# Attention on one core: per-rotation semaphores and group order for the first two heads, other shares of VectorE and GpSimd per head

## The chip, the cores and the metric

The kernel runs on one core of a Trainium2 chip. The metric is the device time of one execution in microseconds (us); the kernel before takes 672.16 us, the median of three runs (672.07 to 673.51). Times inside the kernel come from the profile of one execution, whose span is 670.2 us.

## The reference

Attention with normalised queries and keys: 32 heads, 2048 rows, 20 elements in each row, in bfloat16.

```python
qn = q / (sqrt((q*q).sum(-1)) + eps)
kn = k / (sqrt((k*k).sum(-1)) + eps)
logits = einsum('bhqd,bhkd->bhqk', qn, kn) * t[None, :, None, None]
attn = softmax(logits)
out  = einsum('bhqk,bhkd->bhqd', attn, v)
```

There are 32 x 2048 x 2048 exponentials to take, and a row has only 20 elements, so the exponentials and not the products are the bulk of the work.

## The kernel before, in words

**Units.** Scores are made transposed: keys on the 128 partitions, queries along the free axis. One unit is 128 keys by 512 queries; a head has 16 key blocks r and 4 query groups g, so 64 units. A row has 20 elements, padded to 32, so four of them fit on the 128 partitions: the query tile `qz` is block-diagonal, group g on partitions 32g to 32g+31. A key block r sits on the partitions of group r mod 4. When r mod 4 is not g, the keys must be on other partitions, so three rotated copies of the keys exist (`kR`, rotation dl = (r - g) mod 4 = 1, 2, 3; rotation 0 is `qkT` itself).

**Two engines take exponentials.** Of the 16 key blocks of a head, ScalarE takes 11 or 12 (`A_units`), VectorE 4 or 5 (`D_tiles`, of four units each). The list `DVE_TILES` says how many, by head. ScalarE works in waves of 2 and 3 units in turn: TensorE writes the scores of a wave into one of two slots of `psA`, ScalarE writes the exponentials into the ring `p_ring` (line 757). For VectorE, TensorE writes half a tile, 1024 scores on each of the 128 partitions, into `psD`; VectorE converts it to int16 so that the bits read as float16 are a rough exponential (`xt`, line 803); then three shifts of these integers (`ss`, line 815 on VectorE, line 821 on GpSimd) are combined by TensorE with values `vph` scaled for each shift. There is one `psD` buffer, four `xt` buffers and three of each `ss`. The first two shifts of a tile run on VectorE. The third runs on GpSimd for the first tiles of a head, as many as `KDN` says, and on VectorE for the rest.

**Output.** TensorE accumulates value products of all kinds in `psO` (line 686); when a head is finished, VectorE transposes (line 699), takes the reciprocal of the sum (702), GpSimd or VectorE multiplies (710), and a DMA stores it.

**Preparation of a head.** Loads of q, k and v; squares (527), sums (529), an inverse square root in five or six small steps (532 to 550) on VectorE; the multiplication on GpSimd (562), or on VectorE for heads 1 and 2 (569). Then the SP queue issues a DMA transpose into `qkT` (580), four copies that make `qz`, and six copies that make the three rotations in `kR`, two for each. Head 0 is prepared in its own way, with transposes on TensorE. Heads 1 and 2 are prepared alone, later ones in pairs.

**What sets the order.** All operations are tasks with an engine, an assumed duration, dependences and a due time. When the program is built, `list_schedule` places them with an assumed clock, and each engine then runs its list in that order, in order, with the semaphore waits of `plan_waits`. So a constant of the planner, or a due time, can move instructions anywhere in the kernel. The constants named in the diff: `SWITCH` is a penalty for changing the kind of matmul, `SPARE` the slack that a score matmul must have before it is turned into a slower, fuller form, `DSL` an allowance added to VectorE's backlog when TensorE chooses between scores for ScalarE and for VectorE, `LEAD` how many heads ahead the preparation is due, `DLEAD` how much of a head ahead VectorE's tiles are due.

**Head 0 and the others.** Head 0 visits its units diagonal by diagonal: all units of rotation 0 first, then rotation 1 and so on. The other heads go by key blocks, so their first four units already need all rotations. The semaphore of a copy into `kR` is one for all six (line 590), and the wait of a score matmul is

```python
if h:
    return [trn[h]] + rot[h]      # rot[h]: four qz copies, then six kR copies
```

Of the kernel before, what the change touches and what calls it, by code (L numbers as in the profile page):

```python
# [43 lines left out]
class Program:  # L44
# [2 lines left out]

    SEM_LAT = {"PE": 0.20, "ACT": 0.17, "DVE": 0.14, "POOL": 0.15, "SP": 0.0}

    SWITCH = 0.3  # L50
    LIGHT = 9.0
    TICK = 3.41
    LOAD = 3500.0
# [1 line left out]
    PE_REST = 4.2  # L55
    PV_SLACK = 0.6
    OVER = 0.03
    SPARE = 0.05
    DSL = 0.4
    HOLDA = 9.0  # L60
    HPE = 0.1
    HOLD = {"DVE": 0.0, "PE": HPE}
# [5 lines left out]
    def add(self, eng, name, fn, dur, deps=(), pri=0.0, lat=0.0, dma=None):  # L68
        t = Task(eng, name, fn, dur, deps, pri, lat, dma)
        self.tasks.append(t)  # L70
        return t

    def schedule(self):
# [4 lines left out]
        for _ in range(self.PASSES):  # L78
# [7 lines left out]
            for j, t in enumerate(pe):  # L86
# [3 lines left out]
                for tier in range(3):  # L90
                    m = j - 1
                    while i and load < self.LOAD and m >= i:
                        u = pe[m]
                        if u.modes and u not in heavy and u not in more and (
                                tier == 2 or u.modes[1][2] == u.dur or tier == 1 and
                                u.modes[1][2] - u.dur <= min(v.start for v in u.users) - u.end - 0.2 - self.SPARE):
                            more.add(u)
# [13 lines left out]
    def list_schedule(self):  # L111
# [80 lines left out]
        while events or ready["POOL"]:  # L192
# [13 lines left out]
            for e in touched:  # L206
# [14 lines left out]
                if e == "PE":  # L221
                    if self.DSL is not None and any(r[2].name[0] == "q" for r in ready[e]):
                        more = sum(r[2].dur for r in ready["DVE"]) + self.DSL
                        x = min((r for r in ready[e] if r[2].name[0] == "q"), key=lambda r: (
                            (free["ACT"] if r[2].name[2] == "A" else free["DVE"] + more) - r[2].dur, r[0], r[1]))
                    else:
                        x = min(ready[e], key=lambda r: (r[0] + (0.0 if r[2].name[:2] == last_pe[0] else self.SWITCH), r[1]))
                    ready[e].remove(x)
# [93 lines left out]
def bass_standalone__qk_norm__prompt_kernel(  # L322
# [7 lines left out]
    B, H, S, D = q.shape  # L330
    assert B == 1 and D == 20 and S == 2048, (B, H, S, D)
    R = S // 128
    NG = 4
    WAVES = (2, 3)
    GORD = (0, 2, 1, 3)
# [4 lines left out]
    NV = 6  # L340
# [6 lines left out]
    NWARM = 14  # L347
    EARLY = 3
    NSOLO = 3
    LEAD = 2.9  # L350
    SPREAD = 1.0
    FIRST = -7.0
    DLEAD = 0.9
    PE_MM = 0.23
    MORE = 25
    DVE_TILES = [4 + (h * MORE // 31 > (h - 1) * MORE // 31 if h else 0) for h in range(H)]
    NDMAX = 6
    NPOOL, FPOOL = True, True
    SQPOOL = False
# [1 line left out]
    TTRATE = 0.00168  # L361
    TTDUR, TTWIN = 0.8, 0.55
    NCH = 1
    KDN = (3,)
    PCH, PRATE = 512, 0.00164
    SHP = 0.0

    with ExitStack() as es:
# [11 lines left out]
        vph = [sbuf(f"vph{i}", [128, len(PHASES), NDMAX, 32], FP16) for i in range(NV)]  # L380
# [21 lines left out]
        def dma(eng, name, dst, src, deps, pri, key, lat=2.2, dur=0.65):  # L402
            return add(eng, name, lambda e, tk: e.dma_start(dst, src), dur, deps, pri, lat=lat, dma=key)  # L403
# [5 lines left out]
        A_units, D_tiles = [], []  # L409
        for h in range(H):  # L410
            nd = DVE_TILES[h]
            na = R - nd
            if h == 0:

                A_units += [(0, 4 * c + (g + dl) % 4, g) for dl in range(4) for c in range(3) for g in GORD]
                A_units += [(0, 12 + (g + dl) % 4, g) for dl in range(nd, 4) for g in GORD]
            else:
                A_units += [(h, r, g) for r in range(na) for g in GORD]

            if h == 0:  # L420
                D_tiles += [(0, [12 + (g + dl) % 4 for g in range(NG)]) for dl in range(R - na)]
            else:
                D_tiles += [(h, [r] * NG) for r in range(na, R)]
        NA = len(A_units)
        nA_head = [(R - DVE_TILES[h]) * NG for h in range(H)]
        a0 = [sum(nA_head[:h]) for h in range(H + 1)]
        d0 = [sum(DVE_TILES[:h]) for h in range(H + 1)]
        waves = []
# [32 lines left out]
        lds, ld_v, norm, trn, rot = {}, {}, {}, {}, {}  # L461
# [10 lines left out]
        def add_loads(h):  # L472
            b, bv = h % NB, h % NV
            pri = h - LEAD - 0.5
            war = (norm[h - NB] if h >= NB else []) + ([lambda: [trn[max(0, h - 4)]]] if h >= EARLY else [])
            x = qk_sb[b]
            lds[h] = [dma("SP", f"ldk{h}", x[:, R:2 * R, :], k[0, h].rearrange("(p r) d -> p r d", p=128),
                          war, pri - 0.01 if h else -50, f"k{b}", lat=4.5 if h else 2.2)]
            if h == 0:
                lds[h].append(dma("ACT", "ldq0", x[:, 0:R, :], q[0, 0].rearrange("(p r) d -> p r d", p=128),  # L480
                                  [], -99, "q0a"))
            else:

                for nh in range(4):
                    src = bass.AP(q.tensor, q[0, h].offset + nh * D,
                                  [[16 * D, 32], [4 * D, 4], [512 * D, 4], [1, D]])
                    dst = x[32 * nh:32 * nh + 32, 0:R, :].rearrange("p (c g) d -> p c g d", g=4)
                    lds[h].append(dma("SP", f"ldq{h}", dst, src, war, pri, f"q{b}", lat=4.5))
            war = (pv_users[h - NV] if h >= NV else z_v[bv]) + ([lambda: [trn[h - 2]]] if h >= 2 else [])
            if h == 1:  # L490
                war = war + [lambda: [trn[0]]]
            ld_v[h] = dma("SP", f"ldv{h}", vaug[bv][:, :, 0:D], v[0, h].rearrange("(p r) d -> p r d", p=128),
                          war, pri + 0.1, f"v{bv}", lat=3.0)
            nd = NDMAX if h == 0 else DVE_TILES[h]
            vsc[h] = [add("POOL", f"vs{h}", lambda e, tk, i=i: e.tensor_scalar(  # L495
                vph[bv][:, i, 0:nd, :], vaug[bv][:, R - nd:R, :], 2.0 ** (-PHASES[i] / 1024.0), 1.0, ALU.mult, ALU.mult),
                0.4, [ld_v[h]] + (pv_users[h - NV] if h >= NV else z_v[bv]), pri + 0.2) for i in range(len(PHASES))]
            for u in vsc[h] if h else []:
                u.win = 0.14

        def add_prep(hs):
            due = hs[0] - LEAD if hs[0] != 1 else FIRST
            n = len(hs)
# [72 lines left out]
        def add_trn(h):  # L576
            b, bt = h % NN, h % NT
            due = h - LEAD
            war = [lambda: qk_users[h - NT] + rot[h - NT]] if h >= NT else []
            trn[h] = add("SP", f"trn{h}", lambda e, tk: e.dma_start_transpose(  # L580
                qkT[bt][:, :].rearrange("p (c n) -> p c n", n=128),
                qkn[b][:, :, :].rearrange("p r d -> p (r d)")), 1.3, norm[h] + war, due + 0.1, lat=3.0, dma=f"T{bt}")
            rot[h] = [dma("SP", f"qz{h}", qz[bt][32 * g:32 * g + 32, g, :], qkT[bt][32 * g:32 * g + 32, 0:512],
                          [trn[h], z_qz[bt]] + ([lambda: qk_users[0]] if h == NT else []), due + 0.15, f"Z{bt}") for g in range(NG)]

            for dl in range(1, 4):
                m = 128 - 32 * dl
                for (d, s, n) in ((0, 32 * dl, m), (m, 0, 32 * dl)):
                    rot[h].append(dma("SP", f"rot{h}", kR[bt][d:d + n, dl - 1, :], qkT[bt][s:s + n, 512:1024],
                                      [trn[h]], due + 0.2, f"R{bt}"))  # L590

        warm = []
        for i in range(NWARM):
# [75 lines left out]
        def qk_deps(units):  # L669
            h = units[0][0]  # L670
            if h:
                return [trn[h]] + rot[h]
            return ([head0[0]] if all(r < 8 and r % 4 == g for _, r, g in units) else [trn[0]]) + [q0[g] for _, _, g in units] + [rot[0][dl - 1] for dl in sorted({(r - g) % 4 for _, r, g in units}) if dl]

        first_pv = {}
# [1 line left out]
        def pv_mm(eng, h, r_of, rhs_of, phase=None):  # L677
            start = h not in first_pv
            first_pv[h] = True
            last = None  # L680
            for g in range(NG):
                if phase is None:
                    w = vaug[h % NV][:, r_of(g), :]
                else:
                    w = vph[h % NV][:, phase, r_of(g) - (R - (NDMAX if h == 0 else DVE_TILES[h])), :]
                last = eng.matmul(psO[32 * g:32 * g + 32, :], w, rhs_of(g), start=start,  # L686
                                  stop=False, skip_group_check=True, tile_position=(0, 32 * g))
            return last
# [38 lines left out]
        def add_wave(w):  # L727
# [14 lines left out]
            for h in hs:  # L742
                deps += qk_deps([A_units[u] for u in us if A_units[u][0] == h])
# [31 lines left out]
        def add_dgroup(jg):  # L775
# [5 lines left out]
            for i, j in enumerate(js):  # L781
                h, rg = D_tiles[j]
                due = h + (j - d0[h] + 0.3) / DVE_TILES[h] - DLEAD
                n1 = W1 // 512
# [24 lines left out]
            def dv(name, fn, dur, deps):  # L809
                return add("DVE", f"{name}{js[0]}", fn, 0.068 + dur * len(js), deps, due)  # L810
            sh = []
            for i in range(len(PHASES)):
                dst, war = ss[i][se], t1s + old(f"s{i}", NE)
                if i < 2 or jg < 2 or js[0] - d0[D_tiles[js[0]][0]] >= KDN[D_tiles[js[0]][0] % len(KDN)]:
                    sh.append([dv(f"s{i}.", lambda e, tk, i=i, dst=dst: e.tensor_scalar(  # L815
# [97 lines left out]
```

## Time and profile before

| engine | busy us | share of the span |
|---|---|---|
| TensorE matmul (PE) | 614.8 | 92% |
| VectorE (DVE) | 655.9 | 98% |
| ScalarE (ACT) | 657.3 | 98% |
| GpSimd (POOL) | 350.0 | 52% |

The largest groups of the page: the exponentials on ScalarE (line 757) 650.1 us in 575 instructions; the conversions on VectorE (803) 371.5 us in 306; the shifts on VectorE (815) 242.1 us in 365; the half shifts on GpSimd (821) 234.6 us in 188. In a row of the timeline the columns are start, duration, engine, line, operation, output and input, and in brackets the idle time of the engine before it with what ended that. In a row of the waits they are the engine and line that waited, what it waited for, the total in us, how often, and the longest. In a row by stretches of time they are the busy time of TensorE, its weight loads, VectorE, ScalarE and GpSimd, then the granted TensorE clock as a share of full speed, and the DMA engines' share and rate. The DMA issues of the page give 1.9 us from issue to landing for a `qz` copy and 1.9 to 2.2 us for a `kR` copy.

### The profile page before, as it was taken

To read this page: it belongs to the slowest core of one execution; us is meant where nothing else is said; L and a number is where in the kernel's file an instruction comes from. 1 tells how busy PE (TensorE), PEld (TensorE's weight loads), DVE (VectorE), ACT (ScalarE), POOL (GpSimd) and SP (SyncE) were. 2 spreads that over 40 slices of the span, in tenths; PEclk is the share of its full clock that TensorE was granted. 3 is DMA by queue.
4 is the path that set the end of the run, shared out by engine and by line. 5 is a ranking of instruction groups with operands and counts; after the bars stand their busy time and mean duration, and the time that the engine had idled before them with its cause. 6 is when DMAs were issued, how large, how long until landed. Compare 5 with 4: busy or idle time off the path is not lost.

```text
span 670.2 us, 14522 instructions
## 1 busy us (share of the span) xinstructions
PE 614.8 (92%) x5959; PEld 167.2 (25%) x5959; DVE 655.9 (98%) x927; ACT 657.3 (98%) x584; POOL 350.0 (52%) x364
## 2 busy tenths in 40 slices
PE   8799989999999899899989999999999999999997
PEld 2222222222222222222222222222222222222221
DVE  8979999999999999999999999999999999999997
ACT  9789999999999999999999999999999999999997
POOL 2335555565545546566465645646456456554522
PEclk9979999999999999999999999999999999999999
DMA  5552614425342351333424243352413424130200
GB/s 63 69 76 43 88 18 90 41 57 75 43 80 23 67 64 30 77 36 86 46 48 76 34 85 30 67 65 44 81 17 84 51 41 80 21 86 10 52 8 11
DMA packets 196722, 36.22 MB, mean 54 GB/s; under 512 B 172592, under 2 KB 196656, under 8 KB 196656
## 3 DMA queue, kind: packets, MB, share of 16 engines
q1 hardware_dynamic: 196512, 35.22, 33.7%
q8 instruction: 46, 0.75, 0.5%
q14 instruction: 20, 0.16, 0.1%
q10 hardware_dynamic: 144, 0.08, 0.0%
HBM read 7.87 MB, written 2.62 MB: 16 GB/s over the span
## 4 chain that ended last, share of the span: by engine, by line
ACT 88%; DVE 7%; PE 3%; SPq 1%; DMA 1%; issue 1%
ACT p_ring L757 88%; DVE xt L803 3%; DVE ss L815 2%; PE psA L667 1%; PE psO L594 1%; SPq L403 1%; PE psO L686 1%; DMA qkT<-qkn 0%; PE psD L667 0%; DMA kR<-qkT 0%; DVE rs_sum L529 0%; DVE sq L527 0%; DVE qz L638 0%; DVE oT L699 0%; DVE kx L646 0%
## 5 line engine op out<-in xcount | busy, mean ns | idle before, releaser
L757 ACT ACTIVATE p_ring<-psA 128x1024 bf16<-128x1024 f32 (+1 forms) x575 | 650.1, 1373 | 7.0 <-PE psA L667 7.0
L803 DVE TENSOR_SCALAR xt<-psD 128x1024 int16<-128x1024 f32 x306 | 371.5, 1214 | 7.4 <-PE psD L667 6.5
L821 POOL TENSOR_TENSOR ss<-xt,two 128x512 int32<-128x512 int32 x188 | 234.6, 1248 | 161.4 <-DVE ss L815 80.9
L667 PE MATMUL psA<-qz,kR 32*128 32x512 bf16 (+2 forms) x1077 | 236.8, 386 | 33.6 <-ACT p_ring L757 25.8
L815 DVE TENSOR_SCALAR ss<-xt 128x2048 int16<-128x2048 int16 x365 | 242.1, 683 | 1.2
L686 PE MATMUL psO<-ss,vph 128*32 128x512 f16 x1836 | 171.6, 385 | 0.9 <-DVE ss L815 0.9
L686 PE MATMUL psO<-p_ring,vaug 128*32 128x512 bf16 x1436 | 134.1, 384 | 0.0
L667 PE MATMUL psA<-qz,qkT 64*128 64x512 bf16 (+2 forms) x359 | 121.9, 386 | 10.9 <-ACT p_ring L757 9.4
L667 PE MATMUL psD<-qz,kR 64*128 64x512 bf16 (+1 forms) x459 | 126.1, 386 | 3.9 <-DVE xt L803 2.2
L667 PEld LDWEIGHTS psA<-qz,kR 32*128 32x128 bf16 (+2 forms) x1077 | 55.1, 92 | 184.0 <-ACT p_ring L757 176.4
L495 POOL TENSOR_SCALAR vph<-vaug 128x160 f16<-128x160 bf16 (+2 forms) x96 | 40.2, 419 | 99.7 <-DMA vaug<-in_v_dram 39.0
L686 PEld LDWEIGHTS psO<-ss,vph 128*32 128x32 f16 x1836 | 44.8, 94 | 80.2 <-issue 60.6
L562 POOL TENSOR_TENSOR qkn<-qk_sb,rs_r 128x640 bf16<-128x640 bf16 x29 | 46.8, 1615 | 34.2 <-DVE ss L815 24.2
L686 PE MATMUL psO<-xt,vaug 128*32 128x512 f16 x612 | 60.7, 387 | 0.0
L667 PE MATMUL psD<-qz,qkT 64*128 64x512 bf16 (+1 forms) x153 | 58.6, 387 | 0.8 <-DVE xt L803 0.6
L686 PEld LDWEIGHTS psO<-p_ring,vaug 128*32 128x32 bf16 x1436 | 35.5, 94 | 51.9 <-issue 45.5
L667 PEld LDWEIGHTS psD<-qz,kR 64*128 64x128 bf16 (+1 forms) x459 | 30.4, 93 | 66.8 <-DVE xt L803 50.6
L667 PEld LDWEIGHTS psA<-qz,qkT 64*128 64x128 bf16 (+2 forms) x359 | 29.2, 92 | 58.2 <-ACT p_ring L757 56.7
L710 POOL TENSOR_TENSOR o_stage<-oT,rec 128x320 bf16<-128x320 f32 x30 | 26.0, 866 | 15.3 <-DVE ss L815 12.9
L529 DVE TENSOR_REDUCE rs_sum<-sq 128x32 f32<-128x640 bf16 x32 | 25.5, 802 | 0.1
L686 PEld LDWEIGHTS psO<-xt,vaug 128*32 128x32 bf16 x612 | 15.8, 93 | 34.1 <-issue 26.8
L699 DVE STREAM_TRANSPOSE oT<-psO 128x512 f32<-128x512 f32 x32 | 22.6, 707 | 0.8 <-PE psO L686 0.8
(46 smaller groups left out, 88.9 us busy)
## 6 DMA issues: line engine op xcount, KB each, us to landing
kR<-qkT SPq DMA_DIRECT2D x62, 96.0 KB, 2.2
qz<-qkT SPq DMA_DIRECT2D x124, 32.0 KB, 1.9
kR<-qkT SPq DMA_DIRECT2D x62, 64.0 KB, 2.0
qk_sb<-in_k_dram SPq DMA_DIRECT2D x32, 80.0 KB, 2.2
vaug<-in_v_dram SPq DMA_DIRECT2D x32, 80.0 KB, 4.0
qk_sb<-in_q_dram SPq DMA_DIRECT2D x124, 20.0 KB, 2.5
out_dram<-o_stage SPq DMA_DIRECT2D x31, 80.0 KB, 2.2
kR<-qkT SPq DMA_DIRECT2D x62, 32.0 KB, 1.9
```

What stands on the lines that cost most here:

```text
L403: return add(eng, name, lambda e, tk: e.dma_start(dst, src), dur, deps, pri, lat=lat, dma=key)
L495: vsc[h] = [add("POOL", f"vs{h}", lambda e, tk, i=i: e.tensor_scalar(vph[bv][:, i, 0:nd, :], vaug[bv][:, R - nd:R, :], 2.0 ** (-PHASES[i] ...
L529: sums.append(dv("sum", lambda e, tk, i=i, sqb=sqb: e.tensor_reduce(rs["sum"][:, 2 * R * i:2 * R * (i + 1)], sqb[:, :, :], AXIS_X, ALU.add ...
L562: u = add("POOL", f"norm{h}", lambda e, tk, x=x, b=b, i=i, j=j: e.tensor_tensor(qkn[b][:, j:j + m, 0:D], x[:, j:j + m, :], bc(rs["r"][:, 2 ...
L667: return eng.matmul(dst, lhsT, mov, tile_position=(p0, 0))
L686: last = eng.matmul(psO[32 * g:32 * g + 32, :], w, rhs_of(g), start=start, stop=False, skip_group_check=True, tile_position=(0, 32 * g))
L699: trO[h] = add("DVE", f"tr{h}", lambda e, tk: e.transpose(oT[:, :, :].rearrange("p r d -> p (r d)"), psO[:, :]), 0.63, [lambda: pv_users[h ...
L710: fin[h] = add("POOL" if pool else "DVE", f"fin{h}", lambda e, tk: e.tensor_tensor(st, src, rb, ALU.mult), TTDUR if pool else 0.40, [rc] + ...
L757: act[w] = add("ACT", f"exp{w}", lambda e, tk: e.activation(p_ring[:, p0 * 512:p0 * 512 + n], psA[:, slot * WAVES[0] * 512:slot * WAVES[0] ...
L803: t1_prev[nchunk[0]] = add("DVE", f"t1.{j}.{k}", lambda e, tk, o=o, slot=slot: e.tensor_scalar(xt[sx][:, o:o + W1], psD[:, slot * W1:slot ...
L815: sh.append([dv(f"s{i}.", lambda e, tk, i=i, dst=dst: e.tensor_scalar(dst[:, 0:w], x, float(PHASES[i]), None, ALU.add), 0.533, war)])
L821: u = add("POOL", f"s{i}.{js[0]}.{c}", lambda e, tk, i=i, dst=dst, c=c, n=n: e.tensor_tensor(dst[:, 2 * c:2 * (c + n)].bitcast(I32), xt[sx ...
```

## The change

It has three parts. First, each rotation of a head gets a semaphore of its own, and a score matmul waits only for the rotations that it uses. Second, the first two heads instead of one go diagonal by diagonal, with exactly four VectorE tiles each, so that head 1 can begin with the keys that need no rotation. Third, the shares are placed anew: the heads with four VectorE tiles are 0, 1, 2, 8, 14, 20, 26 (before: 0, 1, 6, 11, 16, 21, 26), and `KDN` is 3 except 2 in heads 15 and 30 and 4 in heads 25 and 29. Five constants of the planner change with it. The purpose is that head 1 need not wait for its whole preparation, and that the engines' loads fit better head by head.

```diff
-    SWITCH = 0.3
+    SWITCH = 0.25
-    SPARE = 0.05
-    DSL = 0.4
+    SPARE = 0.0
+    DSL = 0.8
...
-    LEAD = 2.9
+    LEAD = 3.0
-    DLEAD = 0.9
+    DLEAD = 0.8
-    MORE = 25
-    DVE_TILES = [4 + (h * MORE // 31 > (h - 1) * MORE // 31 if h else 0) for h in range(H)]
+    MORE = 12
+    DLM = 2
+    DVE_TILES = [4, 4, 4, 5, 5, 5, 5, 5, 4, 5, 5, 5, 5, 5, 4, 5, 5, 5, 5, 5, 4, 5, 5, 5, 5, 5, 4, 5, 5, 5, 5, 5]
-    KDN = (3,)
+    KDN = (3, 3, 3, 3, 3, 3, 3, 3, 3, 3, 3, 3, 3, 3, 3, 2, 3, 3, 3, 3, 3, 3, 3, 3, 3, 4, 3, 3, 3, 4, 2, 3)
...
-            if h == 0:
-                A_units += [(0, 4 * c + (g + dl) % 4, g) for dl in range(4) for c in range(3) for g in GORD]
-                A_units += [(0, 12 + (g + dl) % 4, g) for dl in range(nd, 4) for g in GORD]
+            if h < DLM:
+                A_units += [(h, 4 * c + (g + dl) % 4, g) for dl in range(4) for c in range(3) for g in GORD]
-            if h == 0:
-                D_tiles += [(0, [12 + (g + dl) % 4 for g in range(NG)]) for dl in range(R - na)]
+            if h < DLM:
+                D_tiles += [(h, [12 + (g + dl) % 4 for g in range(NG)]) for dl in range(4)]
...
-            nd = NDMAX if h == 0 else DVE_TILES[h]
+            nd = 4 if h < DLM else DVE_TILES[h]
...
-                                      [trn[h]], due + 0.2, f"R{bt}"))
+                                      [trn[h]], due + 0.2, f"R{bt}{dl}"))
...
-                return [trn[h]] + rot[h]
+                return [trn[h]] + rot[h][0:4] + [
+                    rot[h][4 + 2 * dl - 2 + j] for dl in sorted({(r - g) % 4 for _, r, g in units}) if dl for j in range(2)]
```

Before, the scaled values of head 0 were made for six key blocks (`NDMAX`), now for four.

More of the change, by code (lines that the diff above doesn't have):

```diff
@@ L684, in pv_mm @@
                 else:
-                    w = vph[h % NV][:, phase, r_of(g) - (R - (NDMAX if h == 0 else DVE_TILES[h])), :]
+                    w = vph[h % NV][:, phase, r_of(g) - (R - (4 if h < DLM else DVE_TILES[h])), :]
                 last = eng.matmul(psO[32 * g:32 * g + 32, :], w, rhs_of(g), start=start,
```

## The prediction

> **What bounds the kernel now.** I read the page's busy table and its chain first.
>
> ```profile
> PE 614.8 (92%) x5959; PEld 167.2 (25%) x5959; DVE 655.9 (98%) x927; ACT 657.3 (98%) x584; POOL 350.0 (52%) x364
> ACT 88%; DVE 7%; PE 3%; SPq 1%; DMA 1%; issue 1%
> ```
>
> ScalarE (ACT) and VectorE (DVE) both have 98%, and the chain lies on ScalarE. Ledger of ScalarE: the first exponential of the scores starts at 8.62 us, the exponentials are busy 650.1 us (line L757), the waits between them are 7.0 us, the last one ends at 665.76; a tail of 4.4 us (last products, transpose, division, store) makes 670.2. As the exponentials are the same work before and after, what can move is the 7.0. The waits and then the timeline say where it is.
>
> ```profile
> ACT p_ring L757 <- PE psA L667: 7.0, 4, 5.3
> DVE xt L803 <- PE psD L667: 6.5, 12, 2.4
> PE psA L667 <- DMA kR<-qkT: 2.8, 1, 2.8
> ```
> ```profile
> 35.32 2.37 ACT L757 ACTIVATE p_ring<-psA 128x1536 bf16<-128x1536 f32 x2 [5.34 <-PE psA L667]
> 38.11 1.45 ACT L757 ACTIVATE p_ring<-psA 128x1536 bf16<-128x1536 f32 x1 [0.42 <-PE psA L667]
> 40.45 20.45 ACT L757 ACTIVATE p_ring<-psA 128x1024 bf16<-128x1024 f32 x18 [0.89 <-PE psA L667]
> ```
>
> Three of the four waits (5.34 + 0.42 + 0.89 = 6.65 us) stand side by side where head 1 begins, from 29.98 on; one of 0.36 is left for the other 625 us. What ended the first one is in the chain of waits, narrowed to this stretch:
>
> ```profile
> 28.25 0.60 SPq L403
> ...
> 28.89 0.59 SPq L403
> ...
> 31.44 0.59 SPq L403
> ...
> 32.08 2.13 DMA kR<-qkT
> ...
> 34.25 2.00 PE psA L667 x4
> ```
>
> The four copies that make head 1's query tile qz are issued from 26.36 to 28.25, the six that make its rotated keys kR from 28.89 to 32.08; the last of the six lands at 34.21 and lets TensorE (PE) go at 34.25. The small waits after it are its echo, as the table by stretches shows: the granted TensorE clock (the column after POOL) has fallen to half.
>
> ```profile
> 32.00:33.00 1.00, 0.00 (x0) 0.00 (x0) 1.00 (x2) 0.00 (x0) 0.00 (x0) 1.00 0.44 98
> 36.00:37.00 1.00, 1.00 (x3) 0.15 (x1) 0.00 (x0) 1.00 (x2) 0.00 (x0) 0.50 1.13 87
> 40.00:600.00 560.00, 519.57 (x5128) 141.35 (x5130) 556.74 (x772) 559.20 (x495) 311.93 (x305) 1.00 0.36 57
> ```
>
> The last row is the warning: from 40 to 600 us ScalarE idles 0.8 us of 560 (half of it at the edges) and VectorE 3.3. There are two engines at the limit.
>
> [...] TensorE waited for the sixth copy although its first matmul needs none of them. [...] idle from 31.44 to 34.25, clock 0.50 until about 40.2. [...]
>
> **The change part by part.** *Semaphores and group order.* Six copies on one semaphore become three pairs, and head 1's units are walked diagonal by diagonal. The order of the program that results shows it: the wave that holds head 1's first units now waits for the qz copies alone; the next four waves and two VectorE half tiles need unrotated keys only, and the first rotated key comes after them. The last qz copy is issued at 28.25, and a copy of that kind takes 1.9 us to land (page), so at 30.15. From TensorE's start to ScalarE's it was 0.50 us with a full clock (8.12 to 8.62) and 1.07 with half (34.25 to 35.32). TensorE will have idled 0.6 us instead of 2.8, so I take 0.5: the exponential starts at 30.65, a wait of 0.7 us, 1.3 at most with the cold value. The rotated pairs land at about 31.4, 32.8 and 34.2; the first is needed after five waves at 1.13 us (394.39 us for 349 waves in the chain), some 36 us: hidden. With no cold clock the waits of 0.42 and 0.89 go too. **Gain: 6.65 - 0.7 = 5.95 us.** The head-0 products that now stand behind this wave on TensorE's queue are delayed by a microsecond at most; only head 0's transpose waits for them.
>
> *What comes back.* While ScalarE stood 6.65 us, VectorE stood 2.94 (2.40 + 0.30 + 0.24): between 30.9 and 34.7 it did the preparation of heads 3 and 4. So it won 3.7 us on ScalarE, and the later order relies on it. In the new program it wins 0.7 - 0.4 = 0.3 there. Both meet on TensorE, which is in order: a score matmul for VectorE (one psD buffer) waits for VectorE's last conversion, and ScalarE's next wave stands behind it. The other edits must win back 3.4 us. A tile less in head 2 (and one more by head 6) gives ScalarE 4 units more, 4/2.5 x 1.13 = 1.8 us; tiles due 0.1 of a 20 us head later and a larger allowance for VectorE's backlog shift matmuls too. I counted it in both orders: at each half tile (of 306), VectorE's work queued before it, less ScalarE's waves before it, at the median start-to-start times of the trace (waves 1.331 and 0.904, conversion 1.134, shift 0.601, sum 0.726, transpose 0.631, square 0.402, reciprocal 0.163, small ones 0.13). Before and after: half tiles 12 to 118 3.48 and 1.18 (2.3 won, 3.4 needed); 118 to 220 4.12 and -0.05 (4.2 won); 220 to 278 4.85 and 1.79 (3.1); from 278 2.98 and 2.67 (0.3).
>
> So VectorE is 1.1 late early on, 0.8 early in the middle, where it idles, then late again, and 2.8 to 3.1 late at the end, where before it idled 2.9 us after 600 us. If no lateness is forgiven, ScalarE stands 1.1 + 1.1, and about half of the end's idle time is of use, so 1.4 more: 3.6 us. If the one wave that lies ready in psA (1.13 us) forgives the first two, 1.2 remains, all at the end. I take 2.0. **Sum: 5.95 - 2.0 = 3.95 us.**
>
> *At nothing.* Conversions stay 306, VectorE shifts 365, GpSimd half shifts 188, ScalarE waves 574; the tiles per head sum to 153 in both, the shifts kept by head (3, now 2 once in heads 15 and 30, 4 in heads 25 and 29) to 96. One shift moved is 0.6 us of VectorE against two of 1.25 on GpSimd, which is 52% busy; they cancel by the end. Head 0's scaled values shrink from 128x192 to 128x128 on GpSimd early, off the chain. The transpose for head 4 now stands ahead of head 3's copies on the SP queue and waits for head 1's scores: about 52 us (96 units / 2.5 x 1.13, from 8.6), so head 3's keys are there by 63, and head 3 starts near 74. Two more waits per head on TensorE lie on semaphores long reached. The matmul mix hardly moves (171 full-height matmuls into psA become 165, 86 into psD 78).
>
> **The rivals.** *A: the wait is hidden in VectorE's balance, so little comes of it.* For it: VectorE has 98%, and its preparation in the hole was free. If all that VectorE won there (3.4) is paid on ScalarE plus the end's 1.4, the gain is 5.95 - 4.8 = 1.1: 671.0. Against it: VectorE itself idles 14.3 us, of which only about 5 are the start and the tail. *B: slower.* The planner's new constants (no spare for TensorE's slower matmuls, later tiles) leave no slack, and TensorE holds ScalarE up again and again. The trace has one such stop, 0.36 us at 466.8; one every other head is 16 x 0.36 = 5.8, and with the 2.0 above the sum is 7.8 - 5.95 = 1.9 lost: 674.0. Against it: the lag counted falls nearly everywhere, and TensorE's work between two waves is as dense as before. *C: all of it.* The lateness is forgiven, x = 0.2: 666.4.
>
> **How the numbers follow.** The measured median is 672.16, 1.96 above the span; I subtract from it: 672.16 - 3.95 = 668.2. Chances: forecast (667.2 to 669.9) 0.62, A (670 to 671.8) 0.17, B 0.11, C 0.10. The range takes in C's value and most of A: 666.4 to 671.3. Faster by 0.2% is below 670.8: the forecast, C and some two thirds of A, 0.83; the same 0.06 (the rest of A); slower B, 0.11.
>
> **What would show it.** The first wave of head 1 released by the qz copies, ScalarE's wait near 30 us at 0.7 to 1.3 instead of 5.3, no stretch at half clock: this tests the gain. ScalarE's waits for psA in the rest: 0.4 to 3 us, with VectorE's waits for psD fewer after 600 us: this tests what comes back. VectorE's idle time should fall from 14.3 to about 10. The prediction is wrong if ScalarE's waits are scattered over many heads, if a later head waits for its keys, or if the clock still falls at head 1.

## The result and the profile after

The changed kernel takes 668.07 us (median of four, 667.04 to 668.59) against 672.12 (672.04 to 673.51): a ratio of 0.9933, 95% interval 0.9916 to 0.9951, or 4.05 us less. The forecast was 668.2. The profiled run is the fastest of the four, with a span of 665.3 us against 670.2.

The page of the changed kernel, busy table and chain (the score matmuls are line L666 here and L667 before; L757 and L803 are the same):

```profile
PE 601.3 (90%) x5914; PEld 166.3 (25%) x5959; DVE 654.2 (98%) x927; ACT 657.1 (99%) x584; POOL 355.3 (53%) x364
ACT 90%; DVE 5%; DMA 1%; SPq 1%; PE 1%; POOL 0%; issue 0%; ACTq 0%
```

ScalarE's work is what it was; it has become a larger share of a shorter span. Its waits in the changed kernel, and VectorE's (total, times, longest):

```profile
ACT p_ring L757 <- PE psA L666: 2.7, 4, 1.3
DVE xt L803 <- PE psD L666: 3.3, 6, 1.0
```

The 7.0 us have become 2.7. VectorE's idle time, span less busy, falls from 14.3 to 11.1 us. The timeline of the changed kernel near head 1, ScalarE and TensorE:

```profile
30.64 0.37 PE L666 MATMUL psA<-qz,kR 32*128 32x512 bf16 x1 [1.47 <-DMA qz<-qkT]
31.07 22.70 ACT L757 ACTIVATE p_ring<-psA 128x1536 bf16<-128x1536 f32 x20 [1.29 <-PE psA L666]
54.68 5.97 ACT L757 ACTIVATE p_ring<-psA 128x1536 bf16<-128x1536 f32 x5 [0.91 <-PE psA L666]
```

What lets TensorE go is now the query tile and no longer the keys (the first unit of this wave is still head 0's, hence its `kR`). ScalarE waits 1.29 us where it waited 5.34, and then runs 20 waves without a stop. The chain of the changed kernel in the same stretch:

```profile
28.66 1.84 DMA qz<-qkT
30.50 0.14 issue
30.64 0.41 PE psA L666 x3
31.05 0.02 issue
31.07 8.24 ACT p_ring L757 x7
39.31 0.05 issue
39.35 0.60 PE psA L666 x3
39.96 0.23 PE psD L666 x2
40.19 0.02 issue
40.21 1.22 DVE xt L803
```

The end of this excerpt is where something comes back: from 40.21 on, VectorE carries the chain until ScalarE's stop of 0.91 us before 54.68. The table by stretches shows a full clock and busy engines where TensorE stood idle or at half clock before:

```profile
32.00:33.00 1.00, 0.86 (x15) 0.20 (x11) 1.00 (x2) 1.00 (x2) 0.00 (x0) 1.00 0.46 96
36.00:37.00 1.00, 0.73 (x6) 0.10 (x4) 1.00 (x2) 1.00 (x2) 1.00 (x1) 1.00 1.08 74
40.00:600.00 560.00, 512.75 (x5093) 141.18 (x5129) 556.14 (x776) 558.56 (x495) 315.67 (x305) 1.00 0.37 57
```

The ledger of ScalarE closes. First exponential 8.62 to 8.42 (-0.20), exponentials 650.12 to 649.96 (-0.16), waits 7.01 to 2.73 (-4.28), from the end of the last exponential to the end of the span 4.40 to 4.17 (-0.23): together -4.9, the difference of the two spans.

### The profile page after: what moved, and what is told of

Its sections match the earlier page's. It is cut to its first block, busy times and chain, and to the rows that moved or that the text cites. A ratio compares the mean times of both kernels' runs of the same rounds, so it can differ in the third digit from the quotient of the medians.

```text
span 665.3 us, 14541 instructions
## 1 busy us (share of the span) xinstructions
PE 601.3 (90%) x5914; PEld 166.3 (25%) x5959; DVE 654.2 (98%) x927; ACT 657.1 (99%) x584; POOL 355.3 (53%) x364
## 4 chain that ended last, share of the span: by engine, by line
ACT 90%; DVE 5%; DMA 1%; SPq 1%; PE 1%; POOL 0%; issue 0%; ACTq 0%
ACT p_ring L757 89%; DVE xt L803 3%; DVE ss L815 2%; SPq L404 1%; DMA qk_sb<-in_q_dram 1%; DMA qkT<-qkn 0%; ACT qz L450 0%; PE psA L666 0%; PE psD L666 0%; DMA qz<-qkT 0%; POOL qkn L561 0%; POOL ss L821 0%; DVE oT L699 0%; ACT L440 0%; PE psO L686 0%
## 5 line engine op out<-in xcount | busy, mean ns | idle before, releaser
L757 ACT ACTIVATE p_ring<-psA 128x1024 bf16<-128x1024 f32 (+1 forms) x575 | 650.0, 1371 | 2.8 <-PE psA L666 2.7
L803 DVE TENSOR_SCALAR xt<-psD 128x1024 int16<-128x1024 f32 x306 | 371.1, 1213 | 4.4 <-PE psD L666 3.3
L666 PE MATMUL psA<-qz,kR 32*128 32x512 bf16 (+2 forms) x1051 | 227.2, 384 | 36.4 <-ACT p_ring L757 27.7
L666 PE MATMUL psA<-qz,qkT 32*128 32x512 bf16 (+2 forms) x354 | 117.6, 384 | 12.6 <-ACT p_ring L757 10.3
L666 PE MATMUL psD<-qz,kR 64*128 64x512 bf16 (+1 forms) x454 | 120.9, 384 | 7.9 <-DVE xt L803 4.8
L666 PEld LDWEIGHTS psA<-qz,kR 32*128 32x128 bf16 (+2 forms) x1077 | 54.4, 92 | 181.0 <-ACT p_ring L757 176.2
L494 POOL TENSOR_SCALAR vph<-vaug 128x160 f16<-128x160 bf16 (+1 forms) x96 | 40.0, 417 | 80.8 <-DMA vaug<-in_v_dram 39.8
L666 PE MATMUL psD<-qz,qkT 64*128 64x512 bf16 (+1 forms) x144 | 54.3, 385 | 1.4 <-DVE xt L803 0.9
L666 PEld LDWEIGHTS psD<-qz,kR 64*128 64x128 bf16 (+1 forms) x459 | 29.6, 93 | 68.3 <-DVE xt L803 50.8
L666 PEld LDWEIGHTS psA<-qz,qkT 64*128 64x128 bf16 (+2 forms) x359 | 28.5, 92 | 58.4 <-ACT p_ring L757 55.1
L710 POOL TENSOR_TENSOR o_stage<-oT,rec 128x320 bf16<-128x320 f32 x30 | 29.0, 967 | 18.3 <-DVE ss L815 14.3
```

Of the source, the lines that this page charges most:

```text
L666: return eng.matmul(dst, lhsT, mov, tile_position=(p0, 0))
L710: fin[h] = add("POOL" if pool else "DVE", f"fin{h}", lambda e, tk: e.tensor_tensor(st, src, rb, ALU.mult), TTDUR if pool else 0.40, [rc] + ...
L757: act[w] = add("ACT", f"exp{w}", lambda e, tk: e.activation(p_ring[:, p0 * 512:p0 * 512 + n], psA[:, slot * WAVES[0] * 512:slot * WAVES[0] ...
L803: t1_prev[nchunk[0]] = add("DVE", f"t1.{j}.{k}", lambda e, tk, o=o, slot=slot: e.tensor_scalar(xt[sx][:, o:o + W1], psD[:, slot * W1:slot ...
```

## The experiments

The theory: the gain is the wait where head 1 begins, it needs the semaphores and the order together, and the new shares and constants only fit the rest to them. The rival: the shares and constants make the gain. A ratio is to the kernel before on the same chip; its medians on the three chips were 671.42, 672.03 and 671.59. As the chips differ, times of different experiments are compared by their ratios. The expectations were written against 672.16.

### The semaphores alone

```diff
-                                      [trn[h]], due + 0.2, f"R{bt}"))
+                                      [trn[h]], due + 0.2, f"R{bt}{dl}"))
...
-                return [trn[h]] + rot[h]
+                return [trn[h]] + rot[h][0:4] + [
+                    rot[h][4 + 2 * dl - 2 + j] for dl in sorted({(r - g) % 4 for _, r, g in units}) if dl for j in range(2)]
```

> The kernel before with one semaphore per rotation alone; head 1 still goes by key blocks, shares and constants as before. Theory (the gain is the wait where head 1 begins, and it needs semaphores and order together): the first wave of head 1 now waits for rotation 2 only, which landed 1.4 us before the last copy, the second wave for rotation 3, the last; so at most 1 to 1.4 us, 670.7 to 672.1. Rival (the gain comes from the new shares and constants): no change, 672.1 within 0.7.

Measured: 670.87, ratio 0.9991 (0.9982 to 1.0), about 0.6 us. ScalarE's timeline:

```profile
34.66 1.45 ACT L758 ACTIVATE p_ring<-psA 128x1536 bf16<-128x1536 f32 x1 [4.88 <-PE psA L667]
```

Waits of 0.37 and 0.49 follow, and the clock still falls to half (its mean over this run is 0.994). The time fits both forecasts, so it decides nothing here. The profile fits the theory: TensorE goes at 33.59, after the copies of rotation 2 (33.55) and ahead of the last copy (34.95). The wait is shorter by only 0.5 us because the whole queue ran late in this profile: head 1's transpose was issued at 23.86 instead of 23.18.

### The group order alone

```diff
-            if h == 0:
+            if h < DLM:          # DLM = 2; head 1 has four VectorE tiles already
...
```

Head 0's scaled values are then made for four key blocks, as in the change.

> The kernel before with the group order for head 1 alone, one semaphore for all six copies. Theory: head 1's first wave still waits for all six copies, ScalarE stands 5.3 us near 30 and 1.3 more while the clock is at half: 672.1 within 0.7. Rival (the order itself helps, since matmuls of one rotation follow each other): 1 us or more faster.

Measured: 672.02, ratio 1.0007 (1.0 to 1.0015). ScalarE's timeline with the order alone:

```profile
35.64 2.36 ACT L756 ACTIVATE p_ring<-psA 128x1536 bf16<-128x1536 f32 x2 [5.14 <-PE psA L666]
38.24 3.94 ACT L756 ACTIVATE p_ring<-psA 128x1536 bf16<-128x1536 f32 x3 [0.24 <-PE psA L666]
```

The wait is there in full, although the first units need no rotated key. The order alone is worth nothing, for want of a semaphore, and of a wait on it, that tells of less than all six copies.

### Semaphores and order together

Both diffs above, with the shares and constants of before.

> The kernel before with semaphores and group order for head 1, but shares and constants of before. Theory: the wait near 30 falls to 0.7 to 1.3 us and the clock stays full, a gain of about 5.5; VectorE loses its free preparation and ScalarE stands 2 to 4 us elsewhere: 668.2 to 670.2. Rival (shares and constants make the gain): 671.5 to 672.5.

Measured: 667.69 (666.90 to 668.05), ratio 0.995 (0.9932 to 0.9967). That is 3.4 us by the ratio and 3.7 by the medians, near the upper end of the theory's gain of 2.0 to 4.0 us; the rival falls. These two edits hold the gain of the whole change as far as can be told: its ratio of 0.9933 and this one lie in each other's intervals. ScalarE's timeline with both:

```profile
27.80 2.52 ACT L757 ACTIVATE p_ring<-psA 128x1536 bf16<-128x1536 f32 x2
30.81 11.41 ACT L757 ACTIVATE p_ring<-psA 128x1536 bf16<-128x1536 f32 x10 [0.49 <-PE psA L666]
```

The wait is 0.49 us, and one stop of 0.39 is left, at 164.8. So little came back although nothing was done for VectorE's balance.

### Shares and constants without the new order

The changed kernel, with head 1 by key blocks and one semaphore again:

```diff
-    DLM = 2
+    DLM = 1
...
-                                      [trn[h]], due + 0.2, f"R{bt}{dl}"))
+                                      [trn[h]], due + 0.2, f"R{bt}"))
```

and the old wait for all of `rot[h]`.

> The changed kernel with head 1 by key blocks and one semaphore for all six copies as before: the new shares and constants alone. Theory: ScalarE stands 5.3 us near 30 and 1.3 more at half clock as before: 671.5 to 673.5. Rival: most of the 4 us are here, 668 to 669.5.

Measured: 691.3 (690.33 to 692.07), ratio 1.0299 (1.0281 to 1.0317). Neither had it. The rival falls, but the theory's 671.5 to 673.5 is off by 18 us. ScalarE's waits are 17.0 us, 10.0 more than before, 6.9 of the 17.0 at head 1. The rest is at the end: ScalarE's last row and VectorE's last rows in this kernel are

```profile
676.81 1.45 ACT L756 ACTIVATE p_ring<-psA 128x1536 bf16<-128x1536 f32 x1 [0.35 <-PE psA L666]
683.61 1.90 DVE L814 TENSOR_SCALAR ss<-xt 128x2048 int16<-128x2048 int16 x3
687.27 0.49 DVE L709 TENSOR_TENSOR o_stage<-oT,rec 128x320 bf16<-128x320 f32 x1
```

VectorE is done 9.5 us after ScalarE's last wave; before the change it was 2.3. From ScalarE's last wave to the end of the span it takes 11.6 us instead of 4.4. Waits +10.0, this tail +7.2 and exponentials that are 2.3 us longer make 19.5 of the 19.7 by which the span grew. Why the exponentials are longer is open.

This gave a new question: is the tail, which the ledger had held fixed, a matter of the order? The prediction had counted, for each half tile in the program's order, VectorE's queued work less ScalarE's waves; it is a count from the order and mean durations, not a measurement. Averaged over the last 28 half tiles, that lag is 2.98 us before the change and -3.74 here. A negative lag means that VectorE's tiles stand late among ScalarE's waves, so that VectorE is left with work when the waves run out.

### The constants alone, and the shares alone, on top of semaphores and order

```diff
-    SWITCH = 0.3
+    SWITCH = 0.25
...
-    DSL = 0.4
+    DSL = 0.8
```

with `SPARE`, `LEAD` and `DLEAD` as in the change:

> Semaphores, group order and the five planner constants of the change, with the shares (tiles and GpSimd shifts per head) of before. Theory (semaphores and order make the gain; shares and constants are only tuned to each other): the wait near 30 stays under 1.3 us; at the last tiles VectorE's queued work less ScalarE's is -1.7 us here, against 1.8 with semaphores and order alone and 2.7 in the full change, so VectorE ends some 3 to 4 us later: 669.5 to 673. Rival (either half of the retuning is harmless): 667 to 668.7.

Measured: 673.7, ratio 1.0025 (1.0014 to 1.0035). The kernel is slower than before, a little beyond the theory's 669.5 to 673, and the rival's 667 to 668.7 falls. The wait at head 1 stays short (0.47 us), and all waits together are 2.7. ScalarE's last row and VectorE's:

```profile
654.07 8.87 ACT L757 ACTIVATE p_ring<-psA 128x1536 bf16<-128x1536 f32 x8
669.38 0.49 DVE L710 TENSOR_TENSOR o_stage<-oT,rec 128x320 bf16<-128x320 f32 x1
```

ScalarE is through at 662.94, VectorE at 669.87. Against semaphores and order, the span is 6.8 us longer: the tail after ScalarE's last wave 3.9, waits 1.8, longer exponentials 1.0, a later start 0.2. So the tail is the largest part and not the whole.

The new `DVE_TILES` and `KDN`, with the old constants:

> Semaphores, group order and the new shares per head, with the planner constants of before. Theory: as with the constants, and the figure at the last tiles is -3.4 us, near the -3.7 of the kernel with the new shares and constants but the old order, which took 691: 672 to 690. Rival (either half of the retuning is harmless): 667 to 668.7.

Measured: 673.09, ratio 1.002 (1.0013 to 1.0027). This lies at the low end of the theory's wide 672 to 690; the rival falls again. ScalarE ends at 663.02, VectorE at 670.58. The span is 7.5 us longer than with semaphores and order: tail 4.6, waits 2.4, exponentials 1.1, less 0.5 at the start. By the ratios each half of the retuning costs about 5 us when it is alone on the new order; both together cost nothing and gain nothing that these intervals could show.

### One tile less for VectorE at the end

To see whether the tail is VectorE's backlog, the kernel with the constants alone gives one tile of the last head to ScalarE. Its order is the same up to there.

```diff
+    DVE_TILES[31] = 4
```

> Semaphores, group order and the five constants with the shares of before (673.7, where VectorE ended 7 us after ScalarE's last wave), and one VectorE tile of head 31 given to ScalarE; the order up to the last head stays. Theory (what was lost is VectorE's backlog at the end): VectorE loses 4.1 us of work and ScalarE gets 1.8, so VectorE's end comes 1 to 2 us behind ScalarE's: ratio 0.995 to 0.998, 669 to 670.5. Rival (the time was lost by stops on the way): ratio 1.000 to 1.004, since the stops stay and ScalarE has more to do.

Measured: 671.21, ratio 0.9993 (0.9985 to 1.0001), that is 2.2 us of the ratio back (1.0025 to 0.9993). ScalarE's last row and VectorE's transpose in the output:

```profile
654.41 10.77 ACT L758 ACTIVATE p_ring<-psA 128x1536 bf16<-128x1536 f32 x9
665.69 0.72 DVE L700 STREAM_TRANSPOSE oT<-psO 128x512 f32<-128x512 f32 x1 [1.92 <-PE psO L687]
```

VectorE now has to wait 1.92 us for the last products, and ends at 667.22, 2.0 us after ScalarE; the tail is back from 9.1 to 4.7 us. So the tail was VectorE's backlog. But ScalarE ends 2.2 us later than it did, and the ratio lies between the theory's 0.995 to 0.998 and the rival's 1.000 to 1.004. What is left of the loss, against semaphores and order, is in waits (2.2 us more) and in exponentials (3.0 more, of which the tile that ScalarE took over is about 1.8), so the rival has a part in it.

The count and the end of VectorE, for the kernels that give VectorE the same work in sum (the expectations for the constants, for the shares and for the lead of 2.95, the next experiment, already give the count):

| kernel | lag at the last 28 half tiles, us | VectorE's end after ScalarE's last wave, us |
|---|---|---|
| semaphores alone | 3.08 | 2.0 |
| before | 2.98 | 2.3 |
| order alone | 2.98 | 2.3 |
| changed | 2.67 | 2.0 |
| semaphores and order | 1.84 | 3.0 |
| changed, lead 2.95 | 0.82 | 3.6 |
| with constants | -1.68 | 6.9 |
| with shares | -3.35 | 7.6 |
| shares and constants, old order | -3.74 | 9.5 |

From 2.67 down, each smaller count goes with a later end of VectorE. Above that the end stays at 2.0 to 2.3 us; where it is 2.0, VectorE waits for the products of ScalarE's last wave (1.02 us in the changed kernel).

### A new plan by a hair

```diff
-    LEAD = 3.0
+    LEAD = 2.95
```

> The changed kernel with one planner constant moved by a hair (LEAD 2.95 instead of 3.0), which builds the whole order anew. It measures how far a new plan alone moves the time. Theory (the four us are the wait at head 1, in any plan whose figure at the last tiles stays positive; here it is 0.8): 667.5 to 670. Rival (a new plan scatters by many us, and the gain of the change is a lucky plan): above 671.

Measured: 668.68, ratio 0.9947 (0.9932 to 0.9961). The wait at head 1 is 0.82 us, the others 0.66. This is within the theory's 667.5 to 670. Three plans have the gain now, so it is no accident of one.

### What the half clock costs

Ahead of head 1's first wave of the kernel before, TensorE does matmuls of ones into `psD`, which no one reads:

```diff
+            if t.name[:1] == "q" and eng_name == "PE" and t is self.cold:
+                for _ in range(14):
+                    self.dummy(eng)
...
```

`cold` is the first score matmul that waits for head 1's copies.

> The kernel before, with 14 matmuls of ones into psD ahead of head 1's first wave on TensorE, so that TensorE is busy while it would wait; everything else in the same order. Theory (the waits of 0.42 and 0.89 after the long one are the echo of the half clock): the clock stays full, the 5.3 us stay or fall by 0.4, the other two go, 670.3 to 671.2. Rival (they come from VectorE being behind at that point): they stay, 671.5 to 672.5.

Measured: 671.98, ratio 0.9997 (0.9989 to 1.0006). ScalarE's timeline with 14 of them:

```profile
36.46 5.97 ACT L760 ACTIVATE p_ring<-psA 128x1536 bf16<-128x1536 f32 x5 [6.67 <-PE psA L670]
```

The clock stays full (1.00 from 30 to 40 us) and the two small waits are gone, as the theory said of an echo of the half clock. But the time is the rival's, for the long wait has grown by as much: the last copy lands at 35.77 instead of 34.21. With 8 of them:

> The kernel before with 8 instead of 14 matmuls of ones into psD ahead of head 1's first wave. With 14 the clock stayed full, but the last kR copy landed 1.6 us later in that profile and the time did not move. Theory (the late copy was chance, the echo of the half clock is worth about 1 us): 671 to 671.4, ratio 0.998 to 0.999, the small waits gone. Rival (VectorE, not ScalarE, sets the pace there, and the small waits cost nothing): ratio 1.000 within 0.001 with the small waits gone and the copies on time.

Measured: 670.92, ratio 0.9989 (0.9982 to 0.9996), about 0.7 us and as the theory forecast. In the profile the clock fell nevertheless, at 35.99 for 6.8 us, and small waits of 0.21, 0.92, 0.20 and 0.07 followed. But that run, of 672.23 us, is one of the slowest. Of the 20 runs, 15 have a mean clock of 0.999 or 1.0; their median is 670.59. If the clock is either full or half, as in the traces, it was at half in them for some 2 us at most, an estimate from the rounded mean (2 x 0.0015 x 669). The other five have 0.995 or 0.997 and a median of 672.11. All 103 runs of the kernel before have 0.997 or less, and on each of the three chips those with 0.997 are faster than those below it, by 0.6 to 1.0 us.

This is sorting and not an experiment, since copies that land early may make both the stop and the time shorter. With 14 matmuls all 12 runs have 0.999 or 1.0, and yet nothing was gained. So the worth of the half clock stays open, between nothing and the 1.3 us of the two small waits.

### The wait that is left

On the SP queue five loads of head 4 stand before head 1's transpose and copies. In the changed kernel, only these are put behind them:

```diff
+        sp, late = prog.order["SP"], lds[4]
+        sp[:] = [tk for tk in sp if tk not in late]
+        at = sp.index(rot[1][-1]) + 1
+        sp[at:at] = late
...
```

> The changed kernel, with the five loads of head 4 moved on the SP queue from before head 1's transpose and copies to behind them; every other engine's order is the same. Theory (the 1.3 us that are left at head 1 are those loads on the queue): the qz copies land some 2.5 us earlier, ScalarE no longer stands near 31, VectorE waits 1 us less; 0.8 to 1.3 us less than the changed kernel, ratio to the kernel before 0.991 to 0.992. Rival (VectorE's backlog sets the end): ratio 0.993 to 0.994 as for the changed kernel.

Measured: 668.56, ratio 0.9955 (0.9942 to 0.9967). The copies come 3 us earlier and the wait near 31 is gone, as the theory said, but the time has not fallen; it is in neither forecast. VectorE and ScalarE in this kernel:

```profile
37.31 0.49 DVE L526 TENSOR_TENSOR sq<-qk_sb 128x640 bf16<-128x640 bf16 x1 [2.37 <-DMA qk_sb<-in_q_dram]
```
```profile
39.64 1.02 ACT L757 ACTIVATE p_ring<-psA 128x1024 bf16<-128x1024 f32 x1 [1.62 <-PE psA L666]
41.15 2.54 ACT L757 ACTIVATE p_ring<-psA 128x1536 bf16<-128x1536 f32 x2 [0.48 <-PE psA L666]
44.29 2.37 ACT L757 ACTIVATE p_ring<-psA 128x1536 bf16<-128x1536 f32 x2 [0.60 <-PE psA L666]
```

VectorE's squares of head 4 stand in its queue before the next conversions and wait 2.37 us for the load that was put back. TensorE then stands 2.45 us, until 38.99, for the conversion behind them, and ScalarE behind TensorE. The clock falls to half at 40.10 for 3.4 us, and the stops of 0.48 and 0.60 come in this stretch and just behind it. A wait was exchanged for another.

### Both, and less work for VectorE at the end

Semaphores and order with the constants and shares of before, the loads moved, and one shift more on GpSimd in three late heads:

```diff
-    KDN = (3,)
+    KDN = tuple(4 if h in (28, 29, 30) else 3 for h in range(H))
```

> Semaphores and group order with the constants and shares of before, the loads of head 4 behind head 1's copies, and one more GpSimd shift in heads 28, 29 and 30, which takes three shifts of 0.6 us from VectorE: in the profile of semaphores and order alone VectorE ended 3.0 us after ScalarE's last wave. Theory: 0.5 from the copies and 1 to 1.8 from VectorE's end, ratio to the kernel before 0.991 to 0.993. Rival (GpSimd's shifts hold VectorE up as much as they spare it): 0.995 as without.

Measured: 667.04 (665.47 to 667.72), ratio 0.9928 (0.9914 to 0.9941). It is the lowest median of all, but its interval holds the changed kernel's 0.9933. VectorE ends 2.0 us after ScalarE instead of 3.0, and near head 1 ScalarE waits for nothing; stops of 1.11 and 0.51 us near 50 took the place. Two edits were made at once here, so their parts are not told apart.

## Why the prediction was right, step by step

**The gain at head 1.** The mechanism is shown by three runs: order alone and semaphores alone leave the wait at 5.1 and 4.9 us, both together take it to 0.5, and the time falls by 3.4 us in the ratio (0.995). The size was a little high: the query copies landed at 30.50 and not at 30.15, because the transpose before them was issued at 23.49 and not at 23.18 (23.2 to 24.1 in the twelve profiles with the same queue ahead of it). From TensorE's start to ScalarE's it was 0.43 us, near the 0.5 assumed. The wait is 1.29, at the upper end of the 0.7 to 1.3 forecast. The gain is 6.65 - 1.29 = 5.36 instead of 5.95. The rotated pairs landed at 31.8, 33.2 and 34.6, and head 1's first matmul that reads one started at 35.59: hidden, as forecast. "No stretch at half clock" holds for the profile, which is of the fastest run. Two of the four runs have a mean clock of 0.997, that is about 4 us at half by 2 x 0.003 x 666, where the profile has 1.95, all behind 663.32. So in these two the clock fell somewhere; where, no profile shows.

**What comes back.** The sum had 2.0, measured are 1.44 us of waits after head 1 against 0.36 before, so 1.1. The parts: VectorE 1.1 late early on (measured: ScalarE's stops of 0.91, 0.27 and 0.26, the first with VectorE on the chain); VectorE idle in the middle (0.83 and 0.52 us near 290); late again from half tile 220 and at the end: nothing of this. ScalarE ran from 222.7 us to its last wave without a stop. The term that failed is "about half of the end's idle time is of use, so 1.4 more" (it is also the 1.2 that "remains, all at the end", which by the prediction's own figures is 1.4): VectorE's waits for scores after 600 us fell from 2.55 us to 0.69, and no tail came of it.

**"The other edits must win back 3.4 us"** is the step that was wrong in kind. The order of semaphores and order alone wins 1.6, 1.6, 1.4 and 1.1 us in the four sections, and ScalarE's one stop after head 1 was 0.39 us. By the same count a lateness of about 2 us was forgiven, more than the one wave of 1.13 us that the prediction allowed.

**At nothing.** The counts were right (but for the waves, 575 and not 574), but that shares and constants "cancel by the end" holds for the full set only. By the ratios halves of it cost about 5 us each on the new order, the full set on the old order 20.

**The rivals.** A (a gain of 1.1) and C (all of it) did not come. B was rated at 0.11 with scattered stops as its way. The danger was greater than that and lay elsewhere: in the tail, which the ledger had fixed at 4.4 us and which went from 4.2 to 11.6 in these kernels. The count had the figure for it, 2.67 in the changed order against 2.98, and the prediction read it only as a lateness to be paid, not as the thing that keeps the tail short. It gave no reason why the full set should keep the tail short.

**The sum.** 5.95 - 2.0 = 3.95 forecast; by the profiles 5.36 - 1.08 = 4.28, and 0.6 more from the first exponential, the exponentials and the tail in a run that was the fastest of four. Two terms were too large and opposite in sign, so the sum was nearer than its parts: that it came within 0.15 us of the median is luck, while the wait at head 1 is not.

**A reading of the trace.** In the kernel before, GpSimd's shifts wait long for VectorE's:

```profile
POOL ss L821 <- DVE ss L815: 80.9, 73, 7.4
```

These are semaphore waits that the program itself sets: the planner ties each such shift to an instruction of VectorE (`trig`). So they do not show that a shift on GpSimd costs VectorE time by where it is placed. No run here tests that, and the sum does not rest on it.

## What to carry to other kernels

A reordering that lets work begin with what has landed, and a semaphore fine enough to say so, are one change: each alone gained 0.6 us or nothing, both 3.4 to 4. Where two engines share the work and a third feeds both in a fixed order, look at the end of that order too: where one engine's share stood late among the other's, a large part of the loss here was a tail that no wait in the middle showed. And a load that is moved out of a queue's way needs a look at who consumes it next, and where that consumer stands in its own queue.

## What the runs showed that I had not expected

- **The clock fell after short idle stretches.** It went to half with TensorE idle for 2.81 us (before), 2.77 (shares and constants, old order), 2.60 (order alone), 2.45 (loads moved), 2.34 (semaphores alone), 1.89 (with shares), 1.78 (8 matmuls of ones) and 1.45 (loads moved and less for VectorE), and stayed full with 1.47 (changed) and 1.43 (14 matmuls of ones). So the length of the stop alone does not settle it. In the kernel before it fell at 33.41, when TensorE had stood for 1.96 us, and stayed at half for 6.8. In each trace the changes of the clock lie a multiple of 3.41 us apart (before: 27.31, 6.83 and 628.05 us, that is 8, 2 and 184 of them; changed: 658.77, that is 193), so one can ask how busy TensorE is shown in the 3.41 us that end where the clock falls: 20% to 48% in seven of these profiles (23% in the kernel before), 58% in the one with loads moved and less for VectorE. Where it stayed full, the thinnest such stretch ahead of the kernel's end had 54% (14 matmuls), 57% (changed) or more. So the falls and the full clock are not parted by this share either: 58% fell and 54% did not. What decides is not shown. After these stops the half clock lasted 3.4 or 6.8 us each time.
- **A load ahead of a DMA transpose was slow.** With the loads of head 4 moved, the last one, issued at 32.70, 0.7 us ahead of a transpose, landed at 37.28, 4.6 us later, where its neighbours took 2.2 to 2.5; the transpose, issued at 33.38, took 5.2 us, where the one at this place in the changed kernel took 3.4. In the kernel with less for VectorE as well it was 3.8 and 4.4. In the kernel before, a load issued 0.7 us ahead of head 1's transpose took 2.5 and one issued at 24.59, with the transpose in flight, 2.6. So the place alone does not make it slow. The cause was not tried.
- **The plan is sensitive.** With the same work and the same shares, five constants of the planner moved the ratio from 0.995 to 1.0025, about 5 us.
